# Layer 2's first products from seven block products for eight, in blocks of 768 tokens

## The chip, the cores and the metric

The kernel runs on one core of a Trainium2 chip, as one program from DRAM to DRAM. The metric is the device time of that program in microseconds (us). A core has five engines that run their own instruction streams and wait for each other through semaphores: PE (matrix products, which land in the accumulators, PSUM), DVE, ACT and POOL (element by element work on 128 partitions), and SP, which here issues the DMA transfers.

## The reference

Three stages: causal attention with a decay bias, and two layers of the same form. There are 4x8 heads of 576 positions and 64 channels, so 2304 tokens of 512 channels; both layers go to 2048 channels and back.

```python
scores = scale * (q @ k.T);  scores = where(causal, -1e9, scores + min(bias, 0))
x  = softmax(scores) @ v                       # 2304 x 512 after the transpose
h  = x @ w_in                                  # layer 1: 512 -> 2048
g  = h * clip(h + 3, 0, 6) / 6
x  = g @ w_out                                 # 2048 -> 512
h2 = x @ w2_in                                 # layer 2
g2 = h2 * (1 / (1 + exp(-h2)))
out = g2 @ w2_out
```

## The kernel before

**Numbers.** Every float32 operand is kept as a high and a low part in a rounded float32 format (fp32r), and every product is three matmuls, high by high, high by low and low by high, into the same accumulator. The weights arrive as 64-bit words; a chunk (128 rows, 512 KB) is turned into float32 by `Chunk.load`, `fields` (ACT), `join` (three DVE instructions, L146, L150, L153), `high` (ACT) and `low` (DVE, L164), and `Feed.tick` staggers these steps over chunks. A chunk `("i", m, f)` holds the part of layer m+1's first matrix for 128 of the 2048 hidden channels, `("o", m, f)` that of the second matrix.

**Order of work.** Attention goes head by head and is mixed with layer 1, whose 9 blocks of 256 tokens take 8 steps each (16 in block 0), two hidden chunks a step. The list `flat` holds all steps of both layers. For each step `first` multiplies the block's tokens by the chunk (L232 to L234, into `ph`), `gate_high` applies the gate (ACT at L250 in layer 2) and makes the high part (a copy on POOL, L93), `gate_low` the low part (DVE, L255), and `second`, called one step later, adds the product with the second matrix to the block's accumulators (L281 to L283 in layer 2). A scheduler then orders each engine's instructions from what depends on what and on expected times, so the order of the code isn't the order on the engines.

**Layer 2.** It takes the tokens in blocks of 512 (four, and one of 256), 16 steps each, one hidden chunk a step. Between the layers the tokens go through DRAM: `finish1` writes layer 1's result to `x2T_d`, channels by tokens; `load2` and `split2` (L832 to L850) read four pieces of 128 channels for the next block and split them (copies on POOL, L93; subtractions on DVE, L843). `tick2` runs the weights' `Feed` in layer 1's last block, as old chunks come free (`freed`), and on into layer 2. Each step's product goes to one of four one-bank pools `ps_h`, so that `first` can run up to four steps ahead of the gates:

```python
pool = ph_pools[i % len(ph_pools)]
phs[i] = pool.tile([P, len(fs), n], F32, tag="ph", name=f"ph{i}")
```

The main loop of layer 1's last block and of layer 2 is L898 to L911. All of SP's transfers go through one hardware queue.

Of the kernel before, what the change touches and what calls it, by code (L numbers as in the profile page):

```python
# [17 lines left out]
P = 128  # L18
# [4 lines left out]
def f32(ap):  # L23
    return ap.bitcast(F32)
# [3 lines left out]
def kernel(  # L28
# [26 lines left out]
    T1, T2 = 256, 512  # L55
# [4 lines left out]
    wpool = ctx.enter_context(tc.tile_pool(name="wpool", bufs=1))  # L60
    stage = ctx.enter_context(tc.tile_pool(name="stage", bufs=3))
    xpool = ctx.enter_context(tc.tile_pool(name="xpool", bufs=2))
    gpool = ctx.enter_context(tc.tile_pool(name="gpool", bufs=3))
# [3 lines left out]
    ps_acc = ctx.enter_context(tc.tile_pool(name="ps_acc", bufs=2, space=PSUM))  # L67
    ps_h = ctx.enter_context(tc.tile_pool(name="ps_h", bufs=1, space=PSUM))
# [40 lines left out]
    class Chunk:  # L109
        def __init__(self, kind, m, f):  # L110
            self.key = (kind, m, f)
            self.src = ((w1i, w1o), (w2i, w2o))[m][kind == "o"][f]
            self.nm = f"{kind}{m}_{f}"

        def place(self, shape, dt, name):
            kind, m, f = self.key
            return wpool.tile(shape, dt, tag=f"{kind}{f}", name=f"{name}{self.nm}")
# [86 lines left out]
    sizes += [(1, min(T2, NT - t)) for t in range(0, NT, T2)]  # L204
# [6 lines left out]
    xsplit, acc, phs, gs, freed = {}, {}, {}, {}, set()  # L211
    accs_of, finish = {}, {}

    def first(i, j):
# [8 lines left out]
        if blk == NB1 - 1:  # L223
            freed.add(("i", f))
# [11 lines left out]
    def gate_high(i):  # L236
# [7 lines left out]
        if m == 0:  # L244
            nc.scalar.activation(g, ph, AF.Relu, bias=half, scale=1.0 / 6.0)  # L245
            nc.vector.scalar_tensor_tensor(  # L246
                out=g, in0=g, scalar=1.0, in1=ph, op0=ALU.min, op1=ALU.mult
            )
        else:
            nc.scalar.activation(g, ph, AF.Silu)  # L250
# [6 lines left out]
    def second(i, j):  # L257
# [10 lines left out]
        if blk == NB1 - 1:  # L268
            freed.add(("o", f))
# [3 lines left out]
        for t, (a, opens, closes) in outs:  # L273
            cs = slice(t * P, (t + 1) * P)
            b0, b1 = f == 0 and opens, f == NF - 1 and closes
            if m == 0:
                nc.tensor.matmul(a, woh[:, cs], gh[:, jj, :], start=b0, stop=False)  # L277
                nc.tensor.matmul(a, woh[:, cs], gl[:, jj, :], start=False, stop=False)  # L278
                nc.tensor.matmul(a, wol[:, cs], gh[:, jj, :], start=False, stop=b1)  # L279
            else:  # L280
# [690 lines left out]
```

## Time and profile before

| | before |
|---|---|
| median of 3 runs | 1048.12 us (1046.36 to 1048.9) |
| the profiled execution | 1046.25 us |
| its span, first to last instruction | 1044.5 us |
| PE busy | 1014.1 us |
| DVE busy | 600.5 us |
| ACT busy | 437.6 us |
| POOL busy | 273.6 us |
| moved by DMA | 77.10 MB |

The median is the time that is compared. The profile shows one execution, and its span leaves out what lies ahead of the first and behind the last instruction. An engine's busy time is the union of its instructions' times; matmuls are pipelined, so a group's sum of durations can exceed it, and the distance between the starts of two matmuls (the pitch) is what one adds to PE's time. PEclk is the granted clock of TensorE as a share of 2.4 GHz.

### The profile page before, as it was taken

The page shows a single profiled execution, that of the slowest core. Times are in us where ns is not written, and L with a number is a line of the kernel's source. Part 1 is how long each engine was busy: PE and PEld are TensorE (multiplying, and loading weights), DVE is VectorE, ACT ScalarE, POOL GpSimd, SP SyncE. Part 2 cuts the span into 40 slices and gives each one's busy share as a digit, 9 for nine tenths or more (in the row PEclk, how much of TensorE's full clock was granted, in tenths as well). Part 3 has the DMA queues.
Part 4 walks back from the last instruction along what each step waited for, and adds up shares of the span by engine and source line. Part 5 has one row for each costly group of instructions (what it writes and reads, how often), then busy time and mean ns, then how long its engine had stood idle before and what let it go on. Part 6 is the DMA issues. An engine that isn't in the chain of part 4 may idle for free.

```text
span 1044.5 us, 18565 instructions
## 1 busy us (share of the span) xinstructions
PE 1014.1 (97%) x6658; PEld 935.0 (90%) x6658; DVE 600.5 (57%) x1549; ACT 437.6 (42%) x965; POOL 273.6 (26%) x470
## 2 busy tenths in 40 slices
PE   4988999999999999999999999999999999999998
PEld 3778899999999999999999999888888888888897
DVE  6699986878788888888734269992211311211111
ACT  5697744555456666656521157661101111111111
POOL 5000133443244444444402014322111211111100
PEclk9979999999999999999999999999999999999999
DMA  4794121222222322222102268400200100000010
GB/s 149 205 318 139 52 87 43 61 71 58 83 61 61 87 70 59 87 72 57 60 31 68 75 215 289 142 1 11 71 1 0 61 1 1 35 6 1 1 41 21
DMA packets 51428, 77.10 MB, mean 74 GB/s; under 512 B 11796, under 2 KB 34312, under 8 KB 51336
## 3 DMA queue, kind: packets, MB, share of 16 engines
q1 hardware_dynamic: 51336, 75.92, 23.4%
q8 instruction: 53, 0.87, 0.3%
q14 instruction: 39, 0.32, 0.1%
HBM read 65.93 MB, written 9.95 MB: 73 GB/s over the span
## 4 chain that ended last, share of the span: by engine, by line
PE 88%; DVE 7%; DMA 2%; SPq 1%; ACT 1%; issue 1%; POOL 0%; DVEq 0%; ACTq 0%; POOLq 0%
PE ph L232 12%; PE ph L233 12%; PE ph L234 12%; PE acc L281 6%; PE acc L282 6%; PE acc L283 6%; PE acc L277 6%; PE acc L279 6%; PE acc L278 6%; PE poB L598 4%; PE pt0B L549 1%; PE pt1B L549 1%; PE pt2B L549 1%; DVE magi L153 1%; PE ps1B L492 1%
## 5 line engine op out<-in xcount | busy, mean ns | idle before, releaser
L255 DVE TENSOR_TENSOR gl<-g,gh 128x512 fp32r<-128x512 f32 (+1 forms) x152 | 102.3, 674 | 276.9 <-POOL gh L93 276.6
L93 POOL TENSOR_SCALAR gh<-g 128x512 fp32r<-128x512 f32 x136 | 101.7, 749 | 452.9 <-ACT g L250 303.2
L232 PE MATMUL ph<-xh,wi 128*128 128x256 f32 x576 | 167.5, 291 | 5.5 <-DVE g L246 5.4
L278 PE MATMUL acc<-gl,wo 128*128 128x256 f32 x576 | 165.2, 289 | 1.3 <-DVE gl L255 1.3
L233 PE MATMUL ph<-xl,wi 128*128 128x256 f32 x576 | 165.0, 287 | 0.0
L234 PE MATMUL ph<-xh,wi 128*128 128x256 f32 x576 | 165.0, 286 | 0.0
L277 PE MATMUL acc<-gh,wo 128*128 128x256 f32 x576 | 162.5, 288 | 0.8 <-POOL gh L93 0.7
L279 PE MATMUL acc<-gh,wo 128*128 128x256 f32 x576 | 163.2, 285 | 0.0
L250 ACT ACTIVATE g<-ph 128x512 f32<-128x512 f32 x72 | 42.9, 597 | 284.9 <-PE ph L234 284.8
L232 PEld LDWEIGHTS ph<-xh,wi 128*128 128x128 f32 x576 | 111.3, 193 | 7.8 <-DVE g L246 5.8
L233 PE MATMUL ph<-x2l,wi 128*128 128x512 f32 (+1 forms) x320 | 117.7, 368 | 0.0
L234 PE MATMUL ph<-x2h,wi 128*128 128x512 f32 (+1 forms) x320 | 117.7, 368 | 0.0
L232 PE MATMUL ph<-x2h,wi 128*128 128x512 f32 (+1 forms) x320 | 117.7, 368 | 0.0
L278 PEld LDWEIGHTS acc<-gl,wo 128*128 128x128 f32 x576 | 110.2, 191 | 2.9 <-DVE gl L255 2.5
L281 PE MATMUL acc<-wo,gh 128*128 128x512 f32 x288 | 112.3, 390 | 0.0
L282 PE MATMUL acc<-wo,gh 128*128 128x512 f32 x288 | 112.2, 390 | 0.0
L234 PEld LDWEIGHTS ph<-xh,wi 128*128 128x128 f32 x576 | 111.7, 194 | 0.1
L233 PEld LDWEIGHTS ph<-xl,wi 128*128 128x128 f32 x576 | 111.6, 194 | 0.1
L279 PEld LDWEIGHTS acc<-gh,wo 128*128 128x128 f32 x576 | 110.0, 191 | 0.9
L277 PEld LDWEIGHTS acc<-gh,wo 128*128 128x128 f32 x576 | 108.7, 191 | 2.2 <-POOL gh L93 0.9
L283 PE MATMUL acc<-wo,gl 128*128 128x512 f32 x288 | 101.4, 389 | 0.0
L245 ACT ACTIVATE g<-ph,half 128x512 f32<-128x512 f32 (+1 forms) x80 | 51.1, 641 | 64.8 <-PE ph L234 64.7
(197 smaller groups left out, 2107.7 us busy)
## 6 DMA issues: line engine op xcount, KB each, us to landing
k2B<-in_kT_dram SPq DMA_DIRECT2D x64, 144.0 KB
rawi<-in_w1i_dram SPq DMA_DIRECT2D x16, 512.0 KB
rawo<-in_w1o_dram SPq DMA_DIRECT2D x16, 512.0 KB
rawi<-in_w2i_dram SPq DMA_DIRECT2D x16, 512.0 KB
rawo<-in_w2o_dram SPq DMA_DIRECT2D x16, 512.0 KB
q2B<-in_qT_dram SPq DMA_DIRECT2D x64, 80.0 KB
out_dram<-o SPq DMA_DIRECT2D x18, 256.0 KB
vaB<-in_v_dram SPq DMA_DIRECT2D x32, 128.0 KB
```

Of the source, the lines that this page charges most:

```text
L93: nc.gpsimd.tensor_scalar(out=o, in0=i, scalar1=1.0, scalar2=1.0, op0=ALU.mult, op1=ALU.mult)
L232: nc.tensor.matmul(o, wih[:, cs], xh[c], start=c == 0, stop=False)
L233: nc.tensor.matmul(o, wih[:, cs], xl[c], start=False, stop=False)
L234: nc.tensor.matmul(o, wil[:, cs], xh[c], start=False, stop=c == NDC - 1)
L245: nc.scalar.activation(g, ph, AF.Relu, bias=half, scale=1.0 / 6.0)
L255: nc.vector.tensor_tensor(out=gl, in0=g, in1=f32(gh), op=ALU.subtract)
L277: nc.tensor.matmul(a, woh[:, cs], gh[:, jj, :], start=b0, stop=False)
L278: nc.tensor.matmul(a, woh[:, cs], gl[:, jj, :], start=False, stop=False)
L279: nc.tensor.matmul(a, wol[:, cs], gh[:, jj, :], start=False, stop=b1)
L281: nc.tensor.matmul(a, gh[:, jj, cs], woh, start=b0, stop=False)
L282: nc.tensor.matmul(a, gh[:, jj, cs], wol, start=False, stop=False)
L283: nc.tensor.matmul(a, gl[:, jj, cs], woh, start=False, stop=b1)
```

## The change

The first products of layer 2 are made by the scheme of Strassen and Winograd. For a pair q of hidden chunks and a block b of 768 tokens the weights are a 2x2 matrix of blocks (two chunks of 128 hidden channels by two halves of 256 channels), and the tokens another (two halves of 256 channels by two halves of 384 tokens). Eight block products become seven, of sums and differences of blocks, and further sums of the products give the four blocks of the result. There are 3 blocks and 8 pairs, so 24 calls of `step2`, named here step (b,q).

- **Products.** Each of the seven (`product`) is 6 matmuls of 384 columns into one of two PSUM banks in turn. Six more banks hold the accumulators of the second products, which `sums2` adds one step later, 36 matmuls of 512 columns a step, placed between the seven.
- **Sums of products.** Seven additions on DVE (`plus`), each with one operand in PSUM, and one copy on ACT (`p1`). The gate is then four pieces of 384 columns: ACT, POOL, DVE.
- **Sums of weights.** `Two` joins the two chunks of a pair, makes S1 to S4 (four DVE instructions of 256), splits all seven blocks (three copies on ACT and three subtractions on DVE, of 512, 256 and 1024) and writes the result, 128x3584 words, 1.835 MB, to `w7_d` in DRAM. Two buffers hold such results; `again` brings them back two steps ahead of use, 18 times. Pairs 0 to 3 are made in blocks 7 and 8 of layer 1 (in the order 2, 3, 0, 1), pairs 4 to 7 in block 0 of layer 2.
- **Sums of tokens.** `split2(b)` makes the seven token operands of a block: four DVE differences, seven copies on ACT and seven subtractions on DVE, all of 768 words. `x2T_d` now holds the tokens in layer 1's block order, and the output rows are put back in order when they are written.
- **Layer 1** keeps its work; in blocks 7 and 8 the loop is the new one, with four `ph` pools.

The order of all engines is the same, names apart, up to block 7 of layer 1 (some 550 us).

```diff
-    T1, T2 = 256, 512
+    T1 = 256
+    T2, TH = 768, 384
+    w7_d = dram.tile([NF // 2, P, 14 * DM // 2], F32R, tag="w7_d", name="w7_d")
...
+        def sums(self):
+            v = [ch.val for ch in self.ch]
+            (a11, a12), (a21, a22) = [[x[:, :HD], x[:, HD:]] for x in v]
+            self.s = w7pool.tile([P, 4 * HD], F32, tag="s4", name=f"s{self.q}")
+            s1, s2, s3, s4 = [self.s[:, k * HD : (k + 1) * HD] for k in range(4)]
+            for o, x, y, op in (
+                (s1, a21, a22, ALU.add), (s2, s1, a11, ALU.subtract),
+                (s3, a11, a21, ALU.subtract), (s4, a12, s2, ALU.subtract),
+            ):
+                nc.vector.tensor_tensor(out=o, in0=x, in1=y, op=op)
...
+        def split(self):
+            t = w7tile(0, self.q)
...
+            for o, x in parts:
+                nc.scalar.copy(t[:, 0, o], x)
+            for o, x in parts:
+                nc.vector.tensor_tensor(
+                    out=t[:, 1, o], in0=x, in1=f32(t[:, 0, o]), op=ALU.subtract
+                )
+            nc.sync.dma_start(f32(w7_d[self.q]), f32(t.rearrange("p two n -> p (two n)")))
...
+    def again(b, q):
+        t = w7tile(b, q)
+        nc.sync.dma_start(f32(t.rearrange("p two n -> p (two n)")), f32(w7_d[q]))
...
+        parts("b11", b11)
+        minus(b11, b12, b11)
+        t1 = b11
+        minus(b12, b22, b12)
+        t3 = b12
+        parts("b22", b22)
+        minus(b22, b22, t1)
+        t2 = b22
+        parts("t2", t2)
+        parts("b21", b21)
+        minus(b21, b21, t2)
+        t4 = b21
+        parts("t3", t3)
+        parts("t1", t1)
+        parts("t4", t4)
...
+    def product(w, a, name):
...
+        ps = ps_h2.tile([P, TH], F32, tag=f"h{nprod % 2}", name=f"h2_{nprod}")
+        xh, xl = X[name]
+        for c in range(2):
+            cs = slice(a * HD + c * P, a * HD + (c + 1) * P)
+            nc.tensor.matmul(ps, w[:, 0, cs], xh[:, c, :], start=c == 0, stop=False)
+            nc.tensor.matmul(ps, w[:, 0, cs], xl[:, c, :], start=False, stop=False)
+            nc.tensor.matmul(ps, w[:, 1, cs], xh[:, c, :], start=False, stop=c == 1)
+        return ps
...
+        p1 = tile_("p1")
+        x = product(w, A11, "b11")
+        nc.scalar.copy(p1, x)
+        behind(0)
+        u2 = plus("u2", product(w, S2, "t2"), p1)
+        behind(1)
+        h11 = plus("h11", product(w, A12, "b21"), p1)
+        gate(0, 0, h11)
+        behind(2)
+        u3 = plus("u3", product(w, S3, "t3"), u2)
+        behind(3)
+        x = product(w, S1, "t1")
+        h22 = plus("h22", x, u3)
+        gate(1, 1, h22)
+        u4 = plus("u4", x, u2)
+        behind(4)
+        h21 = plus("h21", product(w, A22, "t4"), u3)
+        gate(1, 0, h21)
+        behind(5)
+        h12 = plus("h12", product(w, S4, "b22"), u4)
+        gate(0, 1, h12)
...
+    for n, (b, q) in enumerate(order2):
+        if q == NPAIR // 2 and b + 1 < NB2:
+            load2(b + 1)
+        if q == 0 and b:
+            split2(b)
+        step2(b, q, before)
+        if b == 0:
+            outs2(2 * q + 12)
+            if q + 2 >= EARLY:
+                pair(q + 2)
+        if EARLY <= n + 2 < NPAIR:
+            twos[n + 2].split()
+        elif n + 2 < len(order2):
+            again(*order2[n + 2])
```

(`behind(t)` calls `sums2` for the step before; `gate(i, j, src)` is Silu in place, the POOL copy and the DVE subtraction; `pair` is load, join and sums; `outs2` runs the Feed of the o chunks.)

How the order moves, in two places. First DVE where layer 1 ends. Before, the names are weight chunks (`rawi1_13` and the like are chunk 13 of layer 2's first matrix, `mago` and `wo` stages of the second) and the gates of steps 78 to 80:

```order
L246 SCALAR_TENSOR_TENSOR g79_9469<-g79_9469,ph79_9422 128x512
L146 SCALAR_TENSOR_TENSOR rawo1_9_9709<-rawo1_9_9709 128x512
L153 ISA mago1_2_9355<-rawo1_2_9219,mago1_2_9355 128x1024
L146 SCALAR_TENSOR_TENSOR rawo1_10_9781<-rawo1_10_9781 128x512
L164 TENSOR_TENSOR wi1_4_9353<-magi1_4_9273,wi1_4_9353 128x512
L146 SCALAR_TENSOR_TENSOR rawo1_11_9817<-rawo1_11_9817 128x512
L164 TENSOR_TENSOR wi1_5_9376<-magi1_5_9296,wi1_5_9376 128x512
L255 TENSOR_TENSOR gl79_9471<-g79_9469,gh79_9470 128x512
```

After, `u2`, `h11` and `u3` of step (0,0) (L1006 is `plus`, L152 to L170 are the old L146 to L164) stand in the same place:

```order
L159 ISA mago1_9_9849<-rawo1_9_9700,mago1_9_9849 128x1024
L170 TENSOR_TENSOR wo1_8_9858<-mago1_8_9715,wo1_8_9858 128x512
L1006 TENSOR_TENSOR u2_0_0_9619<-h2_2_9612,p1_0_0_9603 128x384
L156 TENSOR_SCALAR mago1_10_9860<-mago1_10_9860 128x512
L152 SCALAR_TENSOR_TENSOR rawo1_12_9856<-rawo1_12_9856 128x512
L1006 TENSOR_TENSOR h11_0_0_9628<-h2_3_9621,p1_0_0_9603 128x384
L152 SCALAR_TENSOR_TENSOR rawo1_13_9867<-rawo1_13_9867 128x512
L170 TENSOR_TENSOR wo1_9_9986<-mago1_9_9849,wo1_9_9986 128x512
L159 ISA mago1_10_9860<-rawo1_10_9711,mago1_10_9860 128x1024
L156 TENSOR_SCALAR mago1_11_9988<-mago1_11_9988 128x512
L152 SCALAR_TENSOR_TENSOR rawo1_14_9995<-rawo1_14_9995 128x512
L1006 TENSOR_TENSOR u3_0_0_9640<-h2_4_9633,u2_0_0_9619 128x384
```

What moved: additions that empty PSUM banks now stand between stages of the o chunks, where gates stood. Second SP, around the end of layer 1's block 7. Before, it holds loads of layer 2's weights (`in_w2i_dram`) and writes of layer 1's result:

```order
L674 DMA x2T_d_100<-o6_2_8463 128x2x256
L125 DMA rawi1_2_8986<-in_w2i_dram 128x1024
L125 DMA rawi1_3_9039<-in_w2i_dram 128x1024
L125 DMA rawi1_4_9139<-in_w2i_dram 128x1024
L125 DMA rawi1_5_9196<-in_w2i_dram 128x1024
```

After, writes of the weights' sums (`w7_d`) and loads of tokens (`xr`) stand among the loads of weights:

```order
L131 DMA rawi1_0_8740<-in_w2i_dram 128x1024
L872 DMA w7_d_101<-w70_2_8533 128x3584
L131 DMA rawi1_1_8742<-in_w2i_dram 128x1024
L131 DMA rawi1_2_8881<-in_w2i_dram 128x1024
L872 DMA w7_d_101<-w70_3_8676 128x3584
L131 DMA rawi1_3_8883<-in_w2i_dram 128x1024
L905 DMA xr0_0_9022<-x2T_d_100 128x768 x2
L872 DMA w7_d_101<-w70_0_8817 128x3584
L905 DMA xr0_1_9025<-x2T_d_100 128x768 x2
L131 DMA rawi1_8_10008<-in_w2i_dram 128x1024
```

What moved: each write waits for the sums' split on ACT and DVE, and the loads behind it in the queue wait with it.

## Rows read from the trace of the kernel before

**Rows 1.** Page, part 1: busy us, share of the span, instructions.

```profile
PE 1014.1 (97%) x6658; PEld 935.0 (90%) x6658; DVE 600.5 (57%) x1549; ACT 437.6 (42%) x965; POOL 273.6 (26%) x470
```

**Rows 2.** Page, part 2: tenths in 40 slices of the span.

```profile
PE   4988999999999999999999999999999999999998
...
DVE  6699986878788888888734269992211311211111
...
PEclk9979999999999999999999999999999999999999
```

**Rows 3.** Page, part 4: the chain that ended last, by engine.

```profile
PE 88%; DVE 7%; DMA 2%; SPq 1%; ACT 1%; issue 1%; POOL 0%; DVEq 0%; ACTq 0%; POOLq 0%
```

**Rows 4.** PE's waits, 440 to 1045 us.

```profile
engine line waited for: us in total, times, longest us
PE acc L277 <- POOL gh L93: 0.7, 1, 0.7
```

**Rows 5.** Busy time of the engines by stretch (window, its length, engines, clock).

```profile
core 0: us, PE busy (x) PEld busy (x) DVE busy (x) ACT busy (x) POOL busy (x), PEclk, DMA share, GB/s
50.00:60.00 10.00, 8.27 (x33) 7.16 (x32) 10.00 (x32) 10.00 (x26) 0.00 (x0) 0.50 0.94 300
...
50.00:140.00 90.00, 79.10 (x557) 73.86 (x556) 89.79 (x267) 71.05 (x169) 9.89 (x21) 0.90 0.51 166
...
610.00:660.00 50.00, 49.26 (x360) 46.78 (x358) 46.87 (x81) 37.05 (x62) 15.62 (x10) 1.00 0.78 270
660.00:1000.00 340.00, 340.00 (x1517) 282.03 (x1516) 95.48 (x149) 65.74 (x112) 58.18 (x79) 1.00 0.08 25
...
620.00:630.00 10.00, 10.00 (x86) 10.00 (x85) 10.00 (x19) 7.95 (x14) 3.58 (x3) 1.00 0.95 343
```

**Rows 6.** Groups of instructions on PE, shapes kept apart: layer 2's first products.

```profile
L232 PE MATMUL ph<-x2h,wi 128*128 128x512 f32 x256 | 99.7, 389 | 0.0
...
L232 PE MATMUL ph<-x2h,wi 128*128 128x256 f32 x64 | 18.1, 282 | 0.0
```

**Rows 7.** Single matmuls on PE (start, duration), six apart, of 512 and 256 columns.

```profile
699.66 0.39 PE L233 MATMUL ph<-x2l,wi 128*128 128x512 f32 x1
...
701.02 0.39 PE L233 MATMUL ph<-x2l,wi 128*128 128x512 f32 x1
...
1033.38 0.28 PE L233 MATMUL ph<-x2l,wi 128*128 128x256 f32 x1
...
1034.10 0.28 PE L233 MATMUL ph<-x2l,wi 128*128 128x256 f32 x1
```

**Rows 8.** Groups on DVE, shapes kept apart (busy us, mean ns).

```profile
L255 DVE TENSOR_TENSOR gl<-g,gh 128x512 fp32r<-128x512 f32 x136 | 95.8, 705 | 276.9 <-POOL gh L93 276.6
...
L568 DVE TENSOR_TENSOR tl0B<-pt0B,th0B 128x384 fp32r<-128x384 f32 x32 | 17.7, 553 | 1.0 <-ACT th0B L99 0.4
...
L150 DVE TENSOR_SCALAR mago<-mago 128x512 int32<-128x512 int32 x32 | 13.7, 430 | 0.2 <-ACT mago L138 0.2
```

**Rows 9.** Single instructions on DVE, back to back, POOL idle and POOL copying.

```profile
619.50 0.68 DVE L146 SCALAR_TENSOR_TENSOR rawi<-rawi 128x512 int32<-128x512 int32 x1
...
621.30 0.68 DVE L255 TENSOR_TENSOR gl<-g,gh 128x512 fp32r<-128x512 f32 x1
...
664.67 1.10 DVE L164 TENSOR_TENSOR wo<-mago,wo 128x512 fp32r<-128x512 f32 x1
...
666.72 1.09 DVE L255 TENSOR_TENSOR gl<-g,gh 128x512 fp32r<-128x512 f32 x1
```

**Rows 10.** From a product's last matmul through the gate, all engines.

```profile
1034.94 0.28 PE L234 MATMUL ph<-x2h,wi 128*128 128x256 f32 x1
...
1035.26 0.60 ACT L250 ACTIVATE g<-ph 128x512 f32<-128x512 f32 x1 [5.02 <-PE ph L234]
...
1035.94 0.62 POOL L93 TENSOR_SCALAR gh<-g 128x512 fp32r<-128x512 f32 x1 [5.00 <-ACT g L250]
...
1036.59 0.69 DVE L255 TENSOR_TENSOR gl<-g,gh 128x512 fp32r<-128x512 f32 x1 [4.93 <-POOL gh L93]
```

**Rows 11.** The chain that ended last: its first load of 512 KB.

```profile
5.77 6.04 DMA rawi<-in_w1i_dram
```

More of the change, by code (lines that the diff above doesn't have):

```diff
@@ new lines, in step2, with tile_, gate, plus @@
+    def step2(b, q, before):
+        w = W7[b, q]
+        gh, gl = [
+            g2pool.tile([P, 2, T2], F32R, tag=f"{k}{q % 2}", name=f"{k}{b}_{q}")
+            for k in ("gh2", "gl2")
+        ]
+        gates[b, q] = gh, gl
+        def tile_(k):
+            tag, n = ("h", 2) if k[0] == "h" else ("p1" if k == "u4" else k, 1)
+            return g2pool.tile([P, TH], F32, tag=tag, name=f"{k}_{b}_{q}", bufs=n)
+        def gate(i, j, src):
+            g = src
+            nc.scalar.activation(g, src, AF.Silu)
+            o = slice(j * TH, (j + 1) * TH)
+            copy("p", gh[:, i, o], g)
+            nc.vector.tensor_tensor(
+                out=gl[:, i, o], in0=g, in1=f32(gh[:, i, o]), op=ALU.subtract
+            )
+        def plus(name, ps, t):
+            o = tile_(name)
+            nc.vector.tensor_tensor(out=o, in0=ps, in1=t, op=ALU.add)
+            return o
+        def behind(t):
+            if before:
+                sums2(*before, t)
+        p1 = tile_("p1")
[19 more added lines that the diff above has]
+        gate(0, 1, h12)
@@ L888, in tick2 @@
-    def tick2():
-        nonlocal allowed
-        allowed += (2,)[min(step - start, len((2,)) - 1)] / 3
-        while allowed >= 1:
-            allowed -= 1
-            i = feed.t
-            if not feed.done() and (i >= len(keys) or keys[i][::2] in freed):
-                feed.tick()
+    z0 = step
     while step < len(flat):
+        t = step - z0
         first(step, 0)
-        tick2()
+        if t < 2 * EARLY:
+            q = (t // 2 + 2) % EARLY
+            if t % 2 == 0:
+                pair(q)
+            else:
+                twos[q].split()
+        if t == 2 * EARLY:
+            load2(0)
@@ L909 @@
         step += 1
+        if step > first_step[NB1 - 1]:
+            outs2(step - first_step[NB1 - 1])
     second(step - 1, 0)
     second(step - 1, 1)
+    c0.close()
+    g2pool = pool2("g2pool", side="right")
+    ps_a2, ps_h2 = pool2("ps_a2", space=PSUM), pool2("ps_h2", space=PSUM)
+    split2(0)
+    order2 = [(b, q) for b in range(NB2) for q in range(NPAIR)]
+    before = None
+    for n, (b, q) in enumerate(order2):
[12 more added lines that the diff above has]
+            again(*order2[n + 2])
+        before = b, q
+    for t in range(T2 // P):
+        sums2(*before, t)
 def kernel(**inputs):
```

209 lines of the change are left out of this document (116 added, 93 removed).

## The prediction

> **What bounds the kernel now.** I read the busy shares and slices of the page first, then PE's waits in the last 600 us, a table of stretches, and at the end groups and single instructions. PE is busy 97% of the span [rows 1], its granted clock is full outside the first tenth [rows 2], and the chain of waits that ended last is PE for 88% [rows 3]. From 440 us to the end PE waited once, 0.7 us, for a copy on POOL [rows 4]. So a matmul that is left out there is worth its whole pitch, as long as nothing new makes PE wait. The reader is also to see where the other engines have room: between 660 and 1000 us DVE works 95.48 of 340 us, but between 610 and 660 us, where layer 1 hands over to layer 2, 46.87 of 50 us, with the DMA engines 78% busy [rows 5].
>
> **The matmuls.** A matmul's busy time overlaps its successor's, so I price by pitch. Six steps from 699.66 to 701.02 us give 0.227 us for 512 columns, six from 1033.38 to 1034.10 us 0.120 us for 256 [rows 7]. A straight line through both gives 0.173 us for 384, a form that this trace lacks. The first products of layer 2 are now 3x256 of 512 columns and 3x64 of 256 [rows 6]: 768x0.2267 + 192x0.12 = 174.1 + 23.0 = 197.1 us. After the change they are 24 steps x 7 products x 6 = 1008 of 384 columns, 174.7 us. This saves **22.4 us**; bounds are the pitch of 256 scaled by columns (0.180, gain 15.7) and that of 512 scaled (0.170, gain 25.7); the line lies between and I keep it. The 864 second products stay as they are. A new step is 7.28 us of products and 36x0.2267 = 8.16 us of second products, 15.44 us. With the 0.7 us of the old wait gone too, the span would be 1044.5 - 22.4 - 0.7 = 1021.4 us if PE never waited.
>
> **The layer change.** The order of DVE shows what is new: between the first gate of block 8 and the last gate of step (0,1) stand 126 instructions: 71 of 512 words (gates, evacuations, fields of the o chunks, splits; the 18 joined 1024x16-bit ones count here, as they take the time of 512 words), 18 shifts, 4 sums of 256, 11 of 768 (`split2(0)`) and 22 of 384 (`plus` and gates). Back-to-back ones of 512 start 0.60 us apart at 619.50 to 621.30 us [rows 9]; scaled by width, and the shift by 430/705 of a gate [rows 8], that is 71x0.60 + 18x0.37 + 4x0.30 + 11x0.90 + 22x0.45 = 42.6 + 6.7 + 1.2 + 9.9 + 9.9 = 70.3 us. PE's work over the same stretch is 43.2 us of block 8 (8 steps of 48 matmuls of 0.12 us, less the 2.9 us ahead of the first gate), 14 products of 1.04 us and 45 second products of 0.227 us: 68.0 us. In that stretch 16 copies run on POOL. Where such copies ran beside DVE, its instructions started 1.02 us apart (664.67 to 666.72), 0.42 more [rows 9]; at most 16x0.42 = 6.7 us for copies of 512, some 6 as half of them have 384. So DVE needs 70 to 77 us where PE has 68 us of work, and PE waits 2 to 9 us. Every `plus` frees a PSUM bank that the next product but one wants, and there are two banks only: products h2_3 to h2_6 run back to back while u2, h11 and u3 stand between fields of o chunks. The old stretch at 94% DVE lost only 0.7 us, which speaks for the low end; products that can't run ahead speak for more. I take **6 us**, bounds 2 and 14 (DVE's 77 us and 5 us of its own waits for POOL and DMA).
>
> The Trainium skill ("SBUF — State Buffer", "SBUF: two separate sides") says that the port pair shared by VectorE and GpSimd is locked for a whole instruction, the loser blocks fully, and the lock touches only VectorE operations with two SBUF inputs or in a fast mode. The rows' 0.42 us is less than a whole copy of 0.62 [rows 10], so the trace shows a loss, but not all of it. By the page's rule the 16 copies would cost 8.7 us at most in this stretch, and the sum would be 2 us higher; the `plus` of the later steps, which read PSUM, would lose nothing.
>
> **The steady steps.** DVE has 7 `plus` and 4 gates of 384 columns a step: 11x0.45 = 5.0 us, with POOL beside the gates at most 6.7; the weights' sums and splits add some 5 us in steps (0,2) to (0,5). All that is under 15.44 us. ACT has four Silu, one copy and at most three copies of weights, POOL four copies of 384 columns, about 4x0.47 = 1.9 us by width from its 0.62 us [rows 10]. None is the bound. What can cost is the chain behind a bank: the reader starts 0.32 us after the start of a product's last matmul (1034.94 and 1035.26 [rows 10]), some 0.2 us after PE went on; the evacuation takes 0.55 us, as a PSUM-reading DVE instruction of 384 does [rows 8], and I allow 0.1 us for the hand-over back, half of that first one: 0.85 us, against the 1.04 us that the product in the other bank takes. Where two products follow second products this never shows. In every second step four products stand in a row, with gates in DVE's queue between the evacuations; a gate waits Silu, POOL copy and its own start, 1035.26 to 1036.59, 1.33 us [rows 10]. I take 0.1 us for each of some 20 steps, **2 us**, bounds 0 and 6 (0.3 each).
>
> **The block boundaries.** `split2(1)` and `split2(2)` are moved into the step before, 11 DVE instructions of 768 (9.9 us) and 7 copies on ACT beside 5 us of gates; a step's 15.44 us cover that in sum, but the evacuations queue behind 0.90 us pieces, and the six accumulators are read out by ACT and DVE (0.60 us each by DVE's pitch) before the next block's first ones open. I take 1.5 us for each, **3 us**, bounds 0 and 4 each. **The end:** after the last product the last gate's chain (0.95, 0.5, 0.5, 0.5 us by width) runs while second products of other row blocks cover part; I take **1 us**, bounds 0 and 2.5.
>
> **The DMA.** `again` brings back 1.835 MB for each of 18 steps. At the 343 GB/s of 620 to 630 us [rows 5] that is 5.4 us, and what the first 512 KB took beyond their 1.5 us at that rate, 6.04 - 1.5 = 4.5 us [rows 11], makes it 9.9 at most. Its buffer comes free one step of 15.44 us before it is wanted: hidden, at no cost. The writes of the sums stand in SP's one queue ahead of loads of the next chunks; these loads stand a step of layer 1, 5.8 us, ahead of their use, so the writes are hidden too. What each costs if this cover goes is the fourth and the third rival.
>
> **The sum.** 1021.4 + 6 + 2 + 3 + 1 = 1033.4 us of span. The profiled run took 1046.25 us for a span of 1044.5, 1.75 more, and the median of the runs, 1048.12, is 1.87 us over it: 1033.4 + 1.75 + 1.87 = **1037.0 us**, 1.1% faster. With all low ends (gain 25.7, stalls 2) it is 1024; with all high ends (gain 15.7, stalls 30.5) 1062; independent terms rarely meet at an end, so I take half of each distance: 1030 to 1049.
>
> **Rivals.** (1) *The gain comes whole*: the scheduler's order hides the change of layers as the old one did with DVE at 94%. With 3 us of stalls: 1028. For it: rows 4 and 5's 0.7 us lost. Against it: 126 DVE instructions over 68 us and only two banks. 0.17.
>
> (2) *The clock falls*: PE that stops and goes while DVE is full is seen at 50 to 60 us, where PE was 8.27 busy of 10 and the granted clock 0.50, that is 1.2 of 2.4 GHz; from 50 to 140 us DVE was 89.79 of 90 us and the clock 0.90 [rows 5]. If the clock is at 0.50 for 8 us of the layer change, work of 8 us takes 16: 1045, no change that can be told. If layer 2 ran at 0.90 throughout, 370.6 us would become 411.8: 1078, slower. Against it: the pauses of steady steps are tenths of a us in 15.44, and the clock was 1.00 from 610 us with DVE at 94%. 0.10, of it 0.02 for the long one. The Trainium skill ("TensorE: Matmul & The Clock Gate", "A second HAM failure mode: psum-queue depth-cycling") reports a kernel that cycled through PSUM banks, idled briefly between groups and had its clock swing. By that rule the products through two banks would bring the 1078 us. The trace shows full clock where PE cycled through banks without idling [rows 2, 5], and no run here cycles through two of them.
>
> (3) *The writes of the sums hold up the loads, slower than before*: 8 writes of 1.835 MB take 5.4 us each at 343 GB/s and stand in the queue ahead of the weights (order of SP, blocks 7 and 8). ACT's field instructions wait for those weights, and the gates queue behind them on ACT, PE behind the gates. If each write were paid whole: 1021.4 + 43 + 3.6 = 1068. It ends on the slower side once more than 26 of the 43 us are uncovered. For it: the DMA engines were 95% busy when layer 2's weights loaded [rows 5]. Against: 5.4 us is under the lead of 5.8 us, and the loads are now spread over two blocks of 46 us. 0.08.
>
> (4) *The sums come back late*: if 1.835 MB take as long per byte as the first 512 KB, 3.5x6.04 = 21.1 us, each reload is 5.7 us late, 18 times: +103, some 1140. It decides from 15.44 us on; 0.8 us late each is enough for slower. Against: 343 GB/s was reached with 512 KB pieces. 0.05.
>
> **How the numbers follow.** About 3 us, 0.3%, is what a measurement of this kernel can tell from no change: faster is under 1045, slower over 1051. My forecast, 1037 with 1030 to 1049, has 0.60; of that 0.05 lies over 1045. Rivals (1) to (4) have 0.17, 0.10, 0.08 and 0.05. Faster: 0.55 + 0.17 + 0.02 (a still shorter fall) = 0.74; same: 0.05 + 0.06 = 0.11; slower: 0.02 + 0.08 + 0.05 = 0.15. The range of 1026 to 1050 takes the forecast, rival (1) and the short fall of the clock, and leaves out some 0.17.
>
> **What would show it.** First-product matmuls 0.173 us apart, 1008 of them. PE waits for `plus` at the change of layers, 2 to 14 us in all, and next to none for DMA. Steps 15.4 to 15.7 us apart. Clock 1.00 in all of layer 2. Wrong would be: waits for `again` at the start of steps, gates of blocks 7 and 8 late behind loads, a clock under 1.00 after 660 us, or steady steps over 16 us.

## The result, and the profile after

The changed kernel takes 1037.97 us (median of 4 runs, 1036.94 to 1038.37) where the kernel before, run beside it, takes 1047.64; the ratio is 0.9906, 95% interval 0.9889 to 0.9923. The forecast was 1037.0 us, with a range of 1026 to 1050. The number is met, but two of the reasons are not: half of the gain or more comes from a side effect of the change that the prediction had priced at nothing, and the scheme itself gives 1.6 to 5 us of the 11 that were forecast for it. That the total fits is luck.

Page, parts 1 and 2 of the changed kernel (rows as in [rows 1, 2]): PE has 21 us less work, DVE 121 us more, and the DMA engines now move data all through layer 2 (from 660 to 1000 us they are busy for a share of 0.38, before 0.08).

```profile
PE 993.3 (96%) x6706; PEld 937.4 (91%) x6706; DVE 721.5 (70%) x1794; ACT 475.8 (46%) x1042; POOL 264.6 (26%) x474
...
PE   4988999999999999999999998899999999999997
...
DVE  6699986888778888888628889967574343743343
...
PEclk9999999999999999999999999999999999999999
DMA  4793131222222322322114867343354332442412
```

PE's waits from 440 us to the end, the answer to [rows 4] (engine, operation and line, who ended the wait: us in total, times, longest). One wait of 0.7 us has become eleven of 10.2 us. L1006 is `plus`, L1015 the copy `p1`, L98 POOL's copy.

```profile
PE h L951 <- DVE u L1006: 4.1, 6, 1.0
PE h L951 <- ACT p L1015: 3.1, 1, 3.1
PE h L951 <- DVE h L1006: 1.9, 2, 1.0
PE a L967 <- POOL gh L98: 1.0, 2, 0.8
```

Stretches of the changed kernel, columns as in [rows 5] (the clock is the last but two). The change of layers lies now at 640 to 662 us; that is where PE is idle most, and where the clock drops. In the long stretch PE is busy and the clock full.

```profile
640.00:650.00 10.00, 5.91 (x22) 5.09 (x23) 9.42 (x18) 9.93 (x18) 0.72 (x1) 0.83 0.48 188
650.00:660.00 10.00, 8.20 (x40) 6.64 (x39) 10.00 (x20) 5.02 (x9) 1.50 (x3) 1.00 0.51 180
...
660.00:1000.00 340.00, 336.50 (x1670) 301.38 (x1669) 177.05 (x318) 83.68 (x155) 53.79 (x86) 1.00 0.38 138
```

But the two profiles part much earlier. The same 64 matmuls of the attention (those of `poB` with `th0B`; the last two numbers before the semicolon are the first and last start) stand in both kernels in the same place of the order. First the kernel before, then the changed one:

```profile
L598 PE MATMUL poB<-th0B,vsB x64: 212/262/312, 166.6 to 528.0; 128*128 128x320 f32 x32, 128*128 128x64 f32 x32
```

```profile
L591 PE MATMUL poB<-th0B,vsB x64: 207/260/318, 165.2 to 522.0; 128*128 128x320 f32 x32, 128*128 128x64 f32 x32
```

From the first to the last it is 361.4 us before and 356.8 after, with PE busy throughout and the clock at 1.00 in both: 4.6 us less for the same instructions, these 64 and all that lie between them. With 1.4 us from the start, the changed kernel is 6.0 us ahead at a point where nothing that the change describes has begun. From there to the last matmul it gains 6.2 us (1040.30 - 528.09 against 1028.10 - 522.09), and behind the last matmul it loses 2.9 (7.1 us to the end of the span, 4.2 before). That is the question for the experiments: what makes layer 1 faster, and where the forecast 11 us of the scheme went.

### The profile page after: what moved, and what is told of

The parts are those of the page before. It is cut to its first block, busy times and chain, and to the rows that moved or that the text cites. A ratio compares the mean times of both kernels' runs of the same rounds, so it can differ in the third digit from the quotient of the medians.

```text
span 1035.2 us, 19133 instructions
## 1 busy us (share of the span) xinstructions
PE 993.3 (96%) x6706; PEld 937.4 (91%) x6706; DVE 721.5 (70%) x1794; ACT 475.8 (46%) x1042; POOL 264.6 (26%) x474
## 4 chain that ended last, share of the span: by engine, by line
PE 78%; DVE 7%; DMA 7%; POOL 2%; issue 2%; SPq 2%; ACT 1%; DVEq 0%; ACTq 0%; POOLq 0%
PE ph L235 6%; PE acc L275 6%; PE ph L236 6%; PE acc L276 6%; PE ph L237 6%; PE acc L274 6%; PE a L967 5%; PE a L968 5%; PE a L969 5%; PE h L951 5%; PE h L953 5%; PE h L952 5%; PE poB L591 4%; DMA rawi<-in_w1i_dram 2%; DMA out_dram<-o 2%
## 5 line engine op out<-in xcount | busy, mean ns | idle before, releaser
L235 PE MATMUL ph<-xh,wi 128*128 128x256 f32 x576 | 165.7, 288 | 7.8 <-DVE g L248 7.6
L275 PE MATMUL acc<-gl,wo 128*128 128x256 f32 x576 | 163.0, 285 | 0.3 <-DVE gl L255 0.2
L237 PE MATMUL ph<-xh,wi 128*128 128x256 f32 x576 | 163.0, 283 | 0.0
L276 PE MATMUL acc<-gh,wo 128*128 128x256 f32 x576 | 161.3, 283 | 0.0
L274 PE MATMUL acc<-gh,wo 128*128 128x256 f32 x576 | 160.6, 287 | 0.2
L997 ACT ACTIVATE h<-h 128x384 f32<-128x384 f32 x96 | 50.3, 524 | 227.8 <-DVE h L1006 227.2
L98 POOL TENSOR_SCALAR gh<-h 128x384 fp32r<-128x384 f32 x96 | 59.6, 621 | 329.3 <-ACT h L997 329.3
L967 PE MATMUL a<-wo,gh 128*128 128x512 f32 x288 | 113.2, 393 | 1.0 <-POOL gh L98 1.0
L968 PE MATMUL a<-wo,gh 128*128 128x512 f32 x288 | 113.1, 393 | 0.0
L275 PEld LDWEIGHTS acc<-gl,wo 128*128 128x128 f32 x576 | 108.7, 189 | 2.1 <-DVE gl L255 1.7
L274 PEld LDWEIGHTS acc<-gh,wo 128*128 128x128 f32 x576 | 107.3, 189 | 1.7 <-DVE gh L106 0.4
L969 PE MATMUL a<-wo,gl 128*128 128x512 f32 x288 | 96.2, 393 | 0.0
L1000 DVE TENSOR_TENSOR gl<-h,gh 128x384 fp32r<-128x384 f32 x96 | 53.3, 556 | 52.3 <-POOL gh L98 52.1
L98 POOL TENSOR_SCALAR gh<-g 128x512 fp32r<-128x512 f32 x64 | 50.7, 793 | 129.2 <-DVE g L248 115.8
L1006 DVE TENSOR_TENSOR h<-h,u 128x384 f32<-128x384 f32 x72 | 40.0, 556 | 57.9 <-PE h L953 57.5
L248 DVE SCALAR_TENSOR_TENSOR g<-g,ph 128x512 f32<-128x512 f32 (+1 forms) x80 | 50.3, 629 | 38.8 <-ACT g L247 38.6
```

What stands on the lines that cost most here:

```text
L98: nc.gpsimd.tensor_scalar(out=o, in0=i, scalar1=1.0, scalar2=1.0, op0=ALU.mult, op1=ALU.mult)
L235: nc.tensor.matmul(o, wih[:, cs], xh[c], start=c == 0, stop=False)
L237: nc.tensor.matmul(o, wil[:, cs], xh[c], start=False, stop=c == NDC - 1)
L967: nc.tensor.matmul(accs[t], gh[:, k, cs], woh, start=b0, stop=False)
L968: nc.tensor.matmul(accs[t], gh[:, k, cs], wol, start=False, stop=False)
L969: nc.tensor.matmul(accs[t], gl[:, k, cs], woh, start=False, stop=b1)
```

## The experiments

Times stand beside runs of the kernel before on the same chip; where two changed kernels are compared, by their medians. They ran in four groups, and the medians of the kernel before in these and in the result lie between 1045.79 and 1047.64 us (highest beside the changed kernel). So a difference under 2 us between two medians isn't told, and larger ones are given by the ratios to the kernel before as well where that changes them. Unless told otherwise, an edit is made to the changed kernel (1037.97).

**Placement of layer 1's pools (two runs).** The diff puts `xpool` and `gpool` (layer 1's tokens and gates) at the right end of SBUF, to make room for layer 2's pools. It is the one thing in the diff that can touch the matmuls of layer 1 ahead of its block 7. The first run makes this edit alone in the kernel before; no instruction moves.

```diff
-    xpool = ctx.enter_context(tc.tile_pool(name="xpool", bufs=2))
-    gpool = ctx.enter_context(tc.tile_pool(name="gpool", bufs=3))
+    xpool = ctx.enter_context(tc.tile_pool(name="xpool", bufs=2, side="right"))
+    gpool = ctx.enter_context(tc.tile_pool(name="gpool", bufs=3, side="right"))
```

> The kernel before, with one edit that goes with the change but isn't named in it: the pools of layer 1's tokens and gates (xpool, gpool) at the right end of SBUF instead of next to the weights. No instruction and no order changes. Between 146 and 528 us, where the two orders are the same, the profile after is 5 us ahead: back-to-back matmuls of 256 columns are 0.1193 us apart on average, 0.1219 before. Theory A, the placement does this: about 5 to 6 us less, 1041.5 to 1043, mean pitch 0.119 up to 640 us. Theory B, the executions differ by themselves and the placement does nothing: within 0.2% of before (1047.6), mean pitch 0.122.

1041.47 us against 1046.53, ratio 0.9956 [0.9943, 0.9968]. Its profile is that of the slowest of the five executions; in it the change of layers is dearer than in the kernel before (0.7 us, clock 1.00):

```profile
PE acc L277 <- POOL gh L93: 2.5, 1, 2.5
640.00:650.00 10.00, 7.50 (x28) 6.07 (x28) 9.49 (x18) 5.63 (x10) 3.06 (x2) 0.83 0.29 104
```

The second run takes the edit out of the changed kernel (the new pools change sides instead).

```diff
-    xpool = c0.enter_context(tc.tile_pool(name="xpool", bufs=2, side="right"))
-    gpool = c0.enter_context(tc.tile_pool(name="gpool", bufs=3, side="right"))
+    xpool = c0.enter_context(tc.tile_pool(name="xpool", bufs=2))
+    gpool = c0.enter_context(tc.tile_pool(name="gpool", bufs=3))
-    w7pool = pool2("w7pool")
+    w7pool = pool2("w7pool", side="right")
-    g2pool = pool2("g2pool", side="right")
+    g2pool = pool2("g2pool")
```

> The changed kernel with layer 1's pools of tokens and gates where the kernel before has them (next to the weights); the buffers of weight sums go to the right end and layer 2's gates to the left instead. With the run of the kernel before with moved pools (1041.47 against 1046.53, 5.1 us less) this closes the square. Theory A, placement and scheme add: 5 us more than the changed kernel, 1042 to 1044, so that the scheme alone is worth 3 to 4 us; back-to-back matmuls of 256 columns in layer 1 0.122 us apart. Theory B, the gain of the moved pools is one of its particular addresses and the scheme doesn't hang on it: within 1 us of the changed kernel.

1044.89 us against 1046.53, ratio 0.9979 [0.9968, 0.9990]; 6.9 us more than with the edit (7.6 by the ratios), so somewhat over theory A's bound. The same 64 matmuls, first in the kernel before with moved pools, then in the changed kernel with pools back:

```profile
L598 PE MATMUL poB<-th0B,vsB x64: 208/260/318, 166.7 to 523.5; 128*128 128x320 f32 x32, 128*128 128x64 f32 x32
```

```profile
L591 PE MATMUL poB<-th0B,vsB x64: 212/262/312, 167.6 to 529.0; 128*128 128x320 f32 x32, 128*128 128x64 f32 x32
```

356.8 us with the pools moved, 361.4 with the pools in their old place, in either kernel. So placement is shown to be the cause: over this stretch it shortens the mean distance of two successive matmuls of 256 columns from 0.119 to 0.116 us. Most of these distances lie between 0.113 and 0.121 us (those over 0.15, where a record may be missing, are left out); 7% are 0.116 or less with the old placement and 51% with the new one, in either kernel. Which of the operands' addresses does it, and by what, stays open; pools that are opened behind the two may have moved with them. The 1.4 us from the start is something else: with the pools moved in the kernel before, the stretch starts at 166.7 us, as without. The scheme alone is worth 1.6 us with the old placement and 3.5 with the new one (1041.47 to 1037.97); by the ratios it is 2.2 and 5.2.

**What the eighth product would cost.** The first product of a step is made twice.

```diff
-        for c in range(2):
+        for c in range(2) if a != A11 else (0, 1, 0, 1):
```

> The changed kernel with one product more in each step: the product A11 x b11 is made twice into the same bank, the second replacing the first (12 matmuls instead of 6); nothing else is added. This measures what the eighth product costs here. If PE sets the time all through layer 2: 144 matmuls of 384 columns at 0.175 us are 25.2 us, 1062 to 1064, less at most 1 us where it fills pauses. If DVE, ACT or DMA set the pace of the steps, clearly less, under 1055.

1058.32 us, 20.4 more. Steady steps can be read off the copy `p1` on ACT, which comes once a step; first the changed kernel, then with the product more:

```profile
817.98 0.46 ACT L1015 COPY p<-h 128x384 f32<-128x384 f32 x1
...
833.62 0.46 ACT L1015 COPY p<-h 128x384 f32<-128x384 f32 x1
...
849.25 0.46 ACT L1015 COPY p<-h 128x384 f32<-128x384 f32 x1
```

```profile
826.67 0.48 ACT L1015 COPY p<-h 128x384 f32<-128x384 f32 x1 [0.91 <-PE h L953]
...
843.37 0.48 ACT L1015 COPY p<-h 128x384 f32<-128x384 f32 x1 [0.90 <-PE h L953]
...
860.00 0.48 ACT L1015 COPY p<-h 128x384 f32<-128x384 f32 x1 [0.90 <-PE h L953]
```

15.63 us have become 16.67 on average, 1.04 us for 6 matmuls of 384. So PE sets the steady steps alone, and leaving out a product there pays in full. The sum of 24 such steps is 25, and 20.4 by the medians (21.0 between the spans of the two profiles) were paid. What is missing lies mostly in the first block: from step (0,0) to (1,0) the time grows by 5.1 us where eight products take 8.3. PE's waits fall from 10.2 to 8.6 us, and the clock from 640 to 650 us is 1.00 instead of 0.83; what that gives back is worked out below, where the change of layers is compared with its forecast.

**The reloads (two runs).** Without them:

```diff
-        t = w7tile(b, q)
-        nc.sync.dma_start(f32(t.rearrange("p two n -> p (two n)")), f32(w7_d[q]))
+        W7[b, q] = W7[order2[order2.index((b, q)) - 2]]
```

> The changed kernel without the 18 reloads of weight sums; the steps use what stands in the two buffers, so the sums of wrong pairs are multiplied (the same number of matmuls). Steady steps of the changed kernel are 15.63 us apart where the pitches gave 15.44. Theory A, the reloads' traffic into SBUF slows the matmuls: steps of 15.4 us and 3 to 5 us less in all, 1033 to 1035. Theory B, the traffic is free and the longer pitch has another cause: steps of 15.6 us and the same time within 0.2%, 1037 to 1039. Theory C, some reload is waited for: then the gaps at the boundaries of blocks (2.6 us) shrink too.

1039.05 us (1036.78 to 1039.9), steps of 15.62 to 15.65 us: no gain. Theory A falls, the DMA traffic isn't what makes the pitch longer. Theory C isn't borne out either: the wait at the first boundary is longer here, 2.02 us, and the clock falls there:

```profile
780.00:790.00 10.00, 7.99 (x34) 7.36 (x34) 4.78 (x9) 1.94 (x4) 1.53 (x3) 0.83 0.24 94
```

And each made twice:

```diff
+        for _ in range(2):
             nc.sync.dma_start(f32(t.rearrange("p two n -> p (two n)")), f32(w7_d[q]))
```

> The changed kernel with each of the 18 reloads made twice, one behind the other into the same buffer: 3.67 MB a step, 10.7 us at 343 GB/s, where a buffer is free for about 15.6 us. If one reload is well hidden (under 7.8 us), two still are: the same time within 0.2%, no wait of PE for DMA. If the reloads' traffic slows matmuls (theory A of the run without them), 3 to 5 us more. If one reload takes over 8 us, two are late and PE waits for DMA: 18 times the excess, over 1045.

1043.46 us, but over a wide spread (1039.7 to 1046.65, 10 runs). The profiled execution is the fastest of them; in it the steps within blocks 1 and 2 are 15.4 to 16.1 us apart, PE waits once, 0.2 us, for a reload, and 1.6 us more than in the changed kernel, for DVE, just behind the second block boundary.

```profile
PE h L952 <- DMA w<-w_d: 0.2, 1, 0.2
```

Doubled, the reloads cost some 5 us in most executions. Where these lose it, the profile doesn't show; that a single reload is hidden with little room is likely, not shown.

**Layer 2's pool on the other side.**

```diff
-    g2pool = pool2("g2pool", side="right")
+    g2pool = pool2("g2pool")
```

> The changed kernel with the pool of layer 2's gates and partial sums (g2pool) at the left end, next to the buffers of weight sums, instead of at the right end of SBUF. The pitch in steady steps is 0.1753 us for 384 columns and 0.230 for 512, steps 15.63 us. The run of the kernel before with two pools moved showed pitches of 256 columns change by 2% with placement. Theory A, placement sets the pitch here too: steps differ from 15.63 by 0.1 us or more either way, 24 times, 2 us or more in the time. Theory B, the pitch of 512 and 384 columns doesn't hang on this pool's place: steps of 15.6 us and the time within 1 us of the changed kernel.

1037.97 us, steps of 15.69 instead of 15.63 us: a small effect, below what the time can show. With the pools of both layers exchanged (second run above) steps were 15.61, with successive matmuls of 384 columns 0.1734 us apart and those of 512 at 0.227 to 0.234, depending on what follows what. So placement moves single pitches here, too, and the steps' sum hardly.

**The end.** In the changed kernel the last read-outs of accumulators wait for one of two buffers that a DMA still reads. The last matmul and what follows (start, duration, in brackets the idle time before and what ended it):

```profile
1028.10 0.39 PE L969 MATMUL a<-wo,gl 128*128 128x512 f32 x1
1029.49 0.59 ACT L104 COPY o<-a 128x512 f32<-128x512 f32 x1 [2.17 <-DMA out_dram<-o]
1030.30 0.69 DVE L106 COPY o<-a 128x512 f32<-128x512 f32 x1 [2.22 <-DMA out_dram<-o]
```

```diff
-            o = g2pool.tile([P, DM], F32, tag="o", name=f"o{b}_{t}", bufs=2)
+            o = g2pool.tile([P, DM], F32, tag="o", name=f"o{b}_{t}", bufs=4)
```

> The changed kernel with four buffers for output rows instead of two. In the profile after, the last matmul starts at 1028.10 us and the span ends at 1035.2, 7.1 us later (3.9 before); the last two read-outs of accumulators wait 2.2 us each for a buffer that a DMA still reads. Theory A, the two buffers cause this: the last matmul to the end falls to about 4 us and the time by 2.5 to 3.5 us, to 1034.5 to 1035.5 against the changed kernel's 1037.97; the read-outs at the two block boundaries run sooner as well, up to 1 us more. Theory B, the eight issues on SP or the stores themselves set the end: under 0.5 us.

1034.0 us, ratio 0.9884 [0.9868, 0.9899] to the kernel before: 4.0 us less than the changed kernel (2.3 by the ratios, 3.0 between the spans of the two profiles), and the fastest that does all of the work. The last rows are now:

```profile
1026.96 0.40 PE L969 MATMUL a<-wo,gl 128*128 128x512 f32 x1
1027.39 0.69 DVE L106 COPY o<-a 128x512 f32<-128x512 f32 x1 [1.14 <-PE a L969]
```

The span ends at 1032.2, 5.2 us behind the last matmul instead of 7.1 (4.2 in the kernel before, not 3.9): 1.9 us. Another 1.5 come from the first block boundary, where the step falls from 18.13 to 16.64 us, and 0.4 are lost again ahead of the first `p1`. The copies `p1` around the boundary, in the changed kernel and now:

```profile
768.61 0.46 ACT L1015 COPY p<-h 128x384 f32<-128x384 f32 x1
...
786.74 0.46 ACT L1015 COPY p<-h 128x384 f32<-128x384 f32 x1
```

```profile
768.98 0.46 ACT L1015 COPY p<-h 128x384 f32<-128x384 f32 x1
...
785.62 0.46 ACT L1015 COPY p<-h 128x384 f32<-128x384 f32 x1
```

PE's waits for `plus` at this boundary fall from three, 1.7 us, to one of 0.7. That there, too, accumulators waited for read-outs that waited for buffers fits, but was not followed row by row.

**The change of layers (five runs).** ACT's instructions ahead of the first `p1` in the changed kernel, and the wait on PE that it ends:

```profile
639.40 0.67 ACT L143 ACTIVATE rawo<-rawo 128x512 int32<-128x512 uint32 x1 [2.21 <-DMA rawo<-in_w2o_dram]
639.97 0.60 ACT L104 CAST wo<-mago 128x512 fp32r<-128x512 f32 x1
640.48 0.68 ACT L144 ACTIVATE mago<-rawo 128x512 f32<-128x512 f32 x1
641.05 0.57 ACT L104 COPY o<-acc 128x512 f32<-128x512 f32 x1
641.52 0.66 ACT L143 ACTIVATE rawo<-rawo 128x512 int32<-128x512 uint32 x1
642.07 0.62 ACT L104 CAST wo<-mago 128x512 fp32r<-128x512 f32 x1
642.58 0.49 ACT L1015 COPY p<-h 128x384 f32<-128x384 f32 x1
```

```profile
643.12 0.45 PE L951 MATMUL h<-x0b,w 128*128 128x384 f32 x1 [3.13 <-ACT p L1015]
```

The first product was ready before 635 us; its copy stands behind fields of o chunks, one of which waits for its load. The first run takes work of the o chunks away, on ACT and above all on DVE.

```diff
             low, high = self.words
+            if self.key[:2] == ("o", 1):
+                nc.scalar.copy(f32(self.mag), f32(high))
+                self.val = f32(self.mag)
+                return
...
-            if self.src.dtype == F32:
+            if self.src.dtype == F32 or self.key[:2] == ("o", 1):
                 return
```

> The changed kernel in which layer 2's o chunks are not joined from their 64-bit words: of each, ACT copies one of the two words and the three join instructions on DVE are left out (16 ACT and 48 DVE instructions fewer, some 25 us of DVE), the loads stay. In the profile after PE waits 6 us between 640 and 660 us and runs there at a lower clock. Theory A, the o chunks' work on ACT and DVE holds up the copies and additions that empty PSUM banks: PE's waits between 640 and 662 us fall from 6.1 us to 2 or less, and the time by 4 to 7 us. Theory B, the scheme's own chain (p1, u2, u3, then h22, u4 through two banks) is the hold-up: the waits stay at 4 us or more. Theory C, the loads of o chunks are: the same, with waits of ACT for DMA.

1033.07 us, 4.9 less (2.7 by the ratios, 3.7 between the spans). PE's waits from 440 us on, and what held up ACT:

```profile
PE h L955 <- ACT p L1019: 4.7, 1, 4.7
PE h L955 <- DVE u L1010: 2.6, 4, 0.8
PE a L971 <- POOL gh L98: 0.8, 1, 0.8
```

```profile
641.67 0.65 ACT L144 COPY mago<-rawo 128x512 f32<-128x512 f32 x1 [4.54 <-DMA rawo<-in_w2o_dram]
```

The waits for `plus` between 645 and 662 us are gone (the four left lie at the block boundaries), so what theory A says of DVE holds. Its bound doesn't, 2 us of waits or less: the wait for `p1` grows to 4.7, for the reason of theory C, as ACT waits 4.5 us for a load. The clock falls as before (0.83 from 640 to 650 us). Such a load goes into the place of one of layer 1's last chunks: from 600 to 660 us in the changed kernel SP's queue waits 16 times, 29.6 us in all, for matmuls of layer 1's second products ahead of issuing loads of weights.

```profile
SPq L131 <- PE acc L276: 29.6, 16, 8.6
```

The second run moves the copy `p1` to DVE.

```diff
-        nc.scalar.copy(p1, x)
+        copy("v" if (b, q) == (0, 0) else "a", p1, x)
```

> The changed kernel with one instruction moved: the copy p1 of step (0,0) is made by DVE instead of ACT. After, PE waits 3.1 us for this copy, which stands on ACT behind five instructions of o chunks and layer 1's last read-out. Theory A, ACT's queue is what is late: the 3.1 us fall to under 1 and the time by 2 to 3 us. Theory B, DVE is as late as ACT there (94% busy): the wait moves to DVE at 2 us or more and the time stays within 1 us.

1037.23 us; PE waits 3.0 us for the copy on DVE instead, and for the gates' copies 4.5 us, for 1.0.

```profile
PE a L967 <- POOL gh L98: 4.5, 3, 2.3
PE h L951 <- DVE p L106: 3.0, 1, 3.0
```

Theory B: DVE comes to this copy as late as ACT. The third run gives the first six products banks of their own.

```diff
+        if nprod <= 6:
+            ps = ps_a2.tile([P, DM], F32, tag=f"a{nprod - 1}", name=f"h2_{nprod}")[:, :TH]
+        else:
             ps = ps_h2.tile([P, TH], F32, tag=f"h{nprod % 2}", name=f"h2_{nprod}")
```

> The changed kernel in which the first six products of layer 2 go to the six accumulators' banks, which are idle until the sums of step (0,1) begin, instead of to the two banks in turn. Nothing else changes in step (0,0); the order puts its seventh product and the first of step (0,1) ahead, and the six others in a row behind layer 1. Theory B, the two banks are what stops PE at the change of layers: the waits between 640 and 662 us fall from 6.1 us to 2 or less, and the time by 3 us or more, under 1035. Theory A, the queues of ACT and DVE are late by themselves: PE makes the products and then waits as long for the gates of step (0,0) at the first sums; time within 1 us of 1037.97.

1044.45 us, 6.5 more. The premise was wrong, these banks aren't idle: two of them are layer 1's accumulators, and PE now waits for their read-outs, the later of which stands on DVE behind the o chunks:

```profile
PE h L954 <- DVE o L106: 6.1, 1, 6.1
PE a L970 <- POOL gh L98: 5.5, 3, 2.4
PE h L954 <- ACT o L104: 2.6, 1, 2.6
```

These waits and those of rows that are not shown sum to 16.9 us from 440 us on, for 10.2 in the changed kernel, and the clock stays down for longer:

```profile
640.00:650.00 10.00, 1.62 (x7) 1.29 (x8) 8.74 (x16) 9.05 (x16) 0.00 (x0) 0.74 0.47 186
650.00:660.00 10.00, 7.63 (x30) 7.31 (x30) 9.16 (x20) 5.98 (x10) 0.49 (x1) 0.75 0.51 167
```

So the run says nothing on theory B; it shows that the read-outs come late on the same two queues, too. Together with four output buffers it gave:

> The changed kernel with both edits that aim at its own losses: four buffers for output rows and the first six products in the accumulators' banks. The four buffers alone gave 1034.0. If the six banks help as much here as alone, the two add: 1034.0 less what the banks gave, 1031 at best. If the queues are late anyway: 1034 within 0.7 us.

1042.03 us: 2.4 less than with the banks alone, 8 more than with the buffers alone. The last run keeps the four buffers and takes some of DVE's work to POOL.

```diff
-    feed = Feed([("o", 1, f) for f in range(NF)], "a", "v")
+    feed = Feed([("o", 1, f) for f in range(NF)], "a", "vp")
```

> The changed kernel with four buffers for output rows (1034.0 alone) and every other one of the o chunks' low parts made by POOL instead of DVE (8 subtractions of 512). The run without the joins of o chunks took 48 instructions off DVE and 4.9 us off the time, with PE's waits for the partial sums in steps (0,0) and (0,1) gone. Theory A, DVE's load sets the change of layers in proportion: 8 of 48 instructions, about 0.8 us, 1033.2. Theory B, POOL's subtractions slow DVE as its copies do (0.42 us each for one of 512, more with two inputs) and hold up the gates' copies behind them on POOL: 1034 to 1036. Theory C, the wait for p1, which ACT makes behind loads of o chunks, is alone what counts: no change, 1034.0 within 0.5.

1035.01 us (1034.49 to 1038.87), 1.0 more than the four buffers alone: theory B by its bounds, though within the runs' spread. The profile is that of the slowest execution, 3.9 us over the median, so it can't explain the median. Against the profile of the four buffers alone it loses 3.6 us before 169 us, where the edit changes nothing but the clock is lower (0.77 from 50 to 100 us, for 0.93). From 440 us on its waits for `p1` and `plus` are 1.8 and 2.8 us (4.1 and 5.1 there), but the last gates of layer 1 now come late (rows of L274 and L275), and from 650 to 660 us the clock is 0.66, for 1.00.

```profile
PE h L951 <- DVE u L1006: 2.4, 4, 0.7
PE acc L275 <- DVE gl L255: 1.8, 1, 1.8
PE h L951 <- ACT p L1015: 1.8, 1, 1.8
PE acc L274 <- POOL gh L98: 1.1, 1, 1.1
```

## Why the prediction was right, and where it was right by luck

**The matmuls, 22.4 us: right in mechanism, 4.6 us too much.** The steady step came out at 15.63 us for 15.44. From 802 to 896 us, matmuls of 384 columns lie 0.1753 us apart (0.1733 by the line from [rows 7]) and those of 512 0.230 (0.2267): 42 x 0.0020 + 36 x 0.0031 = 0.20 us a step, all of the difference. (In block 0 the steps are 13.9 to 17.0 us apart, but the eight take 126.0 us, 1.0 more than eight of 15.63.) Neither the reloads (first run without them) nor pauses (product made twice) cause it. The pitch of 512 columns was taken over from other operands in other places, and pitches of 256 columns were seen to change with place by 2.6%; that this is the cause here is likely, not shown.

**The steady steps, 2 us of pauses: too much.** There is one, 0.89 us in block 0; between 800 and 900 us PE didn't wait once. The bank arithmetic (0.85 us against 1.04) holds; what was missing in the steps is in the pitch.

**The change of layers, 6 us: right place and size, wrong first culprit.** The waits from 640 to 662 us sum to 3.13 + 0.96 + 0.76 + 1.04 + 0.21 = 6.1 us. The step had DVE finishing late behind 126 instructions; DVE is 21.0 of 22 us busy there, and with 48 of its instructions gone the waits for `plus` vanish. But the first and longest wait is ACT's, behind a load of an o chunk. The step gave ACT no term; waits of ACT for loads stand only in rival (3), and the load's place is free only when layer 1 is nearly through. Besides, the clock fell behind this wait: from 644.10 to 647.60 us the ten distances between successive matmuls of 384 columns sum to 3.50 us (seven are 0.32), where ten of 0.1753 are 1.75: some 1.7 us lost. This is rival (2) in small, at a fifth of its price. With a product made twice the clock didn't fall there; its 1.7 us, and 1.7 us less of waits, are most of the 4.0 us that the profile of that run doesn't pay.

**The block boundaries, 3 us: right.** The waits are 0.78 + 0.65 + 0.26 = 1.7 us at the first and 0.7 at the second, 2.4 in all. That a part of it came from the two output buffers was not seen.

**The end, 1 us with bounds 0 and 2.5: wrong.** The wait that was priced is there (0.82 us), but what follows the last matmul takes 2.9 us more than before. Six row blocks go out through two buffers, where the kernel before had one for each; with four buffers 1.9 of the 2.9 us are gone, and the other 1.0 stays open. The diff showed `bufs=2`; the step looked only at the chain of the last gate.

**Layer 1, nothing: wrong, by 5 to 7 us to the good.** The prediction took the equal order of instructions as equal time up to 550 us. The diff's move of two pools was read as housekeeping. This term hid the others: with the forecast 11.1 us of the scheme the total would have been some 1031; without the move the measured 1044.9 is within the range, too, but is a change of 0.2%, no gain to speak of. From the kernel before with moved pools to the changed kernel the scheme gives 3.5 us by the medians and 5.2 by the ratios, where the steps said 11. The profile of the changed kernel accounts for 7.3 us of the shortfall: 4.6 for the pitches, 1.7 for the clock and 2.7 at the end, against 1.7 us of pauses in steps and at boundaries that didn't come. That leaves 3.8 us (an estimate, as the kernel with moved pools has waits of its own at the change of layers).

**The rivals.** (1), with DVE's lateness hidden, fell: 10.2 us of waits. (2) fell for layer 2: at 660 to 1000 us the clock is 1.00, though products go through two banks in turn and PE paused six times, 0.2 to 0.9 us each. The rule of the Trainium skill on cycling through PSUM banks ("TensorE: Matmul & The Clock Gate", "A second HAM failure mode: psum-queue depth-cycling") does not show in this stretch. Where the clock did drop, at 640 to 650 us, PE was busy 5.91 of 10 us, and ahead of the drop it had waited 3.1 us in one piece; the run without reloads had such a drop in layer 2 too, once, behind a wait of 2.0 us. (3) fell: in layer 1's blocks 7 and 8 PE lost next to nothing (50.00 of 50 us from 560 to 610, 29.93 of 30 from 610 to 640), though ACT did wait for loads. (4) fell: PE waits for no reload, and two in a row were just about hidden in the one profile there is, that of the fastest of ten executions.

## What to carry to other kernels

Leaving out matmuls pays its full pitch where PE is the only engine that is late, and that can be read from one run with a product made twice. What it costs is at the seams: at a change of layers the instructions that empty accumulators stand in queues filled by preparation for later, some of it waiting for loads, and at the end too few store buffers; count each engine's waits there, not only its busy time. And compare two kernels first over a stretch that the change shouldn't touch: if it moved, something else did, such as where pools lie.

## What was not expected of the hardware

The place of operands in SBUF changes the rate of matmuls whose clock is full and which wait for nothing: the stretch from the first to the last of the same 64 attention matmuls takes 361.4 us with one placement and 356.8 with the other, in two kernels each, and in it successive matmuls of 256 columns of fp32r lie 0.119 or 0.116 us apart on average. Moving 1.835 MB of reloads a step, or none, made no difference to the matmuls (steps of 15.63 us in both).
